# Dealing the rows of w_out four to a partition, and taking h's weights from every fourth column of w_in

## The chip, the cores and the metric

The kernel runs on one core of a Trainium2 chip. A core has a matrix engine (TensorE; the profile writes PE for its matmuls and PEld for its weight loads), a vector engine (DVE), a scalar engine (ACT), GpSimd (POOL), a queue engine that only issues transfers (SP), and 16 DMA engines that carry all transfers. The metric is the device time of one execution in microseconds (us).

## The reference

Two steps follow each other. The first is a gated linear attention over 4 batches, 8 heads, 768 positions and a head size of 48: a state of 48 x 48 per head is faded by a sigmoid gate, receives the outer product of k and v, and is read with q. The second is a feed-forward layer whose activation is a ratio of polynomials, on the 3072 x 384 rows that the first one gives.

```python
f = 1.0 / (1.0 + np.exp(-f_logit))
for t in range(S):
    state = f[:, :, t, :, None] * state + np.einsum('bhd,bhe->bhde', k[:, :, t], v[:, :, t])
    y[:, :, t] = np.einsum('bhd,bhde->bhe', q[:, :, t], state)
...
h = x @ w_in                       # 3072 x 384 by 384 x 2048
h2 = h * h
P = a[0] + a[1] * h + a[2] * h2 + a[3] * h2 * h
Q = 1.0 + np.abs(b[0]) * np.abs(h) + np.abs(b[1]) * h2
out = (P / (Q + 1e-06)) @ w_out    # 2048 x 384
```

The 2048 columns of h (the ff dimension) are independent of each other up to the last product, which sums over them. Any dealing of them to blocks and partitions gives the same output if w_in and w_out follow it alike.

## The kernel before, in words

The work is cut into 12 units of 256 positions (4 batches times 3 chunks). A unit goes through the attention part (steps ef, ls, cs, A, xa, T, sc, mk, yi, yb, ic, si, st, ye) and gives x, 256 tokens by 384, transposed, in bf16. Then the feed-forward part runs on it:

- h (line 480): 16 blocks of 128 ff columns. For each block three matmuls run over the 384 rows of w_in (three tiles of 128). The weights are 128 columns of w_in, the moving operand is x with 256 columns. A step h takes four blocks, thus 12 matmuls, into one PSUM slot; 12 units give 48 steps and 576 matmuls.
- hy (line 492, ACT) brings four blocks from PSUM to SBUF as bf16. The polynomials are made of it by DVE and ACT (sq, sa, ab, p1, p2, pm, tv, zv, gm, and the reciprocal rq), and some of their additions by DMAs that GpSimd issues and that add into their destination (zd, line 514, into z; ta, line 543, into g).
- o (line 560): 16 blocks again. The weights are 128 tokens of g for one ff block, the moving operand is the 384 columns of w_out for the same block. 384 matmuls in all.
- oe (line 568) scales the result, so (line 577) stores it.

All elementwise work treats the ff columns alike, so which column lies in which block or on which partition does not matter to it.

The order of all steps is written out by hand in the string ORDER; each engine runs its own instructions in that order and waits on semaphores for what it needs from others. Marks such as `!m3` and `^m3` tie a step behind another one. There are four PSUM slots; the `@` numbers name the slot.

Both weight matrices stay in SBUF in bf16 and are loaded once by GpSimd's queue, which converts them from float32 on the way: w_in by eight transfers (wi, line 218), w_out by four (wo, line 224). A wo step brings four blocks, thus 512 rows of w_out. In ORDER they stand as wo 8 12, then later wo 4 8, wo 12 16 and wo 0 4, all always in whole groups of four blocks. Before the change, partition p of block m holds row 128 m + p of w_out, so one transfer is, for each of the 128 partitions, four separate runs of one row (384 values). Block m of h takes the packed columns 128 m to 128 m + 127 of w_in.

Of the kernel before, what the change touches and what calls it, by code (L numbers as in the profile page):

```python
# [104 lines left out]
def _at(t, dims, off=0):  # L105

    return bass.AP(tensor=t.tensor, offset=t.offset + off, ap=[t.ap[0]] + [list(d) for d in dims])
# [3 lines left out]
def kernel(  # L111
# [15 lines left out]
    P = 128  # L127
    HP = H // 2
    DM = H * D
    d_ff = moe_w_in.shape[1]  # L130
# [36 lines left out]
    w_in_sb = consts.tile([P, KD, d_ff], BF16, name="w_in_sb")  # L167
# [22 lines left out]
    def unit(n):  # L190
        if n not in units:
            c, b = divmod(n, B)
            units[n] = dict(n=n, c=c, b=b, qk=qkp[n % 2], ls=lsp[n % 2], vm=vmp[n % 2])
        return units[n]
# [5 lines left out]
    def slot(i, shape, dtype, name):  # L200
        return slots[i].tile(shape, dtype, name=name, tag="s")
# [19 lines left out]
                                        ap=[[d_ff, 32], [32 * d_ff, KD], [1, n]]))  # L221

    def load_w_out(m0, m1):
        return nc.gpsimd.dma_start(out=w_out_sb[:, m0:m1, :],
                            in_=moe_w_out[m0 * P:m1 * P, :].rearrange("(ko ki) n -> ki ko n", ki=P))

    def load_ab(what, qu="a"):
        dst, src = (a_sb, moe_a) if what == "a" else (b_sb, moe_b)
# [19 lines left out]
    def const_z(i):  # L248
        if i < 2:
            nc.vector.memset(lsp[i][:, :, :, D:E], 0.0)  # L250
            nc.vector.memset(qkp[i].rearrange("p x i h d -> p (x i h) d")[:, :, D:E], 0.0)
            nc.vector.memset(vmp[i][:, :, :, 16:32], 0.0)
        elif i == 2:
            nc.vector.memset(ind, 0.0)
            for j in range(UB):
                nc.vector.memset(ind[R * j:R * j + R, j, :], 1.0)
        elif i == 4:
            return nc.vector.memset(zz, 0.0)
        else:
            nc.vector.memset(hsel, 0.0)  # L260
            for r in range(2):
                nc.vector.memset(hsel[E * r:E * r + E, :, :, 1 - r], 1.0e4)
# [212 lines left out]
    def h(n, m0, m1, sl):  # L475
        s = unit(n)
        t = s["hp", m0] = slot(sl, [P, 4, NT], F32, "hp")
        for m in range(m0, m1):
            for kk in range(KD):
                nc.tensor.matmul(t[:, m - m0, :].rearrange("f (j t) -> f j t", j=UB),  # L480
                                 w_in_sb[:, kk, m * P:(m + 1) * P], s["x"][:, :, kk, :],
                                 start=(kk == 0), stop=(kk == KD - 1))

    def big(s, key):
# [94 lines left out]
    def behind(i, mark):  # L579
        tc.add_manual_dep(i.ins, marks[mark].ins.name,  # L580
                          mybir.DependencyInfo(mybir.DependencyClass.Sync, mybir.DependencyReason.DATA),
                          reason="begins behind it")

    steps = dict(ld=load, wi=load_w_in, wo=load_w_out, ab_=load_ab, cu=const_u, ci=const_i, cm=const_m,
                 cz=const_z, fa=coef_a, fb=coef_b, fr=coef_r, tab=tab, dm=dm, ef=ef, ls=ls, cs=cs, A=A, xa=xa, T=T, Te=Te,
                 sc=sc, mk=mk, vm=vm, yi=yi, yb=yb, ic=ic, si=si, ye=ye, st=st, h=h, hy=hy, sq=sq, sa=sa, ab=ab,
                 zv=zv, zd=zd, rq=rq, p1=p1, p2=p2, pm=pm, ta=ta, tv=tv, gm=gm, o=o, oe=oe, so=store)
    for step in ORDER.replace("\n", ";").split(";"):
# [41 lines left out]
```

## Time and profile before

| | |
|---|---|
| median of 3 runs | 220.51 us (218.54 to 227.84) |
| the profiled execution | 219.54 us |
| its span, first to last instruction | 217.8 us |
| TensorE matmuls busy | 194.5 us, 2901 instructions |
| TensorE weight loads busy (beside the matmuls) | 138.5 us, 2902 instructions |
| DVE busy | 190.6 us |
| ACT busy | 187.5 us |
| GpSimd busy | 78.8 us |
| matmuls of h (line 480) | 576, 70.9 us |
| weight loads of h | 576, 55.7 us |
| matmuls of o (line 560) | 384, 69.2 us |
| four transfers of w_out | 384 KB each in SBUF, 8.4 us from issue to landing in the median |

Busy time is the time that an engine's instructions cover. A matmul's shown length contains latency that overlaps with the next one, so a row's mean is longer than the distance from one matmul to the next; the distance is read from rows that put several together. The loads of weights run beside the matmuls and have a row of their own. For a transfer the profile gives the time that the issuing engine is occupied and, separately, the time from issue to landing.

### The profile page before, as it was taken

The page shows a single profiled execution, that of the slowest core. Times are in us where ns is not written, and L with a number is a line of the kernel's source. Part 1 is how long each engine was busy: PE and PEld are TensorE (multiplying, and loading weights), DVE is VectorE, ACT ScalarE, POOL GpSimd, SP SyncE. Part 2 cuts the span into 40 slices and gives each one's busy share as a digit, 9 for nine tenths or more (in the row PEclk, how much of TensorE's full clock was granted, in tenths as well). Part 3 has the DMA queues.
Part 4 walks back from the last instruction along what each step waited for, and adds up shares of the span by engine and source line. Part 5 has one row for each costly group of instructions (what it writes and reads, how often), then busy time and mean ns, then how long its engine had stood idle before and what let it go on. Part 6 is the DMA issues. An engine that isn't in the chain of part 4 may idle for free.

```text
span 217.8 us, 6636 instructions
## 1 busy us (share of the span) xinstructions
PE 194.5 (89%) x2901; PEld 138.5 (64%) x2902; DVE 190.6 (88%) x243; ACT 187.5 (86%) x178; POOL 78.8 (36%) x98
## 2 busy tenths in 40 slices
PE   1397699699988899999999999999999999999791
PEld 0355478477756766666678668768677757765440
DVE  4178549999999999999999999999999999979960
ACT  3863639979989999999999999999999999998921
POOL 7050724116394074070260055193553414132000
PEclk9999889999999999999999999999999999999999
DMA  6999997599899979999999999999999999999722
GB/s 171 232 313 168 253 240 189 66 297 182 217 187 178 163 113 200 223 213 191 253 197 164 257 241 243 210 193 204 215 204 199 221 199 215 207 205 199 158 72 72
DMA packets 61820, 43.15 MB, mean 198 GB/s; under 512 B 51424, under 2 KB 56544, under 8 KB 61792
## 3 DMA queue, kind: packets, MB, share of 16 engines
q0 software_dynamic: 20528, 23.86, 66.9%
q1 hardware_dynamic: 41264, 18.88, 33.2%
q8 instruction: 22, 0.36, 0.6%
q14 instruction: 6, 0.05, 0.1%
HBM read 25.17 MB, written 4.72 MB: 137 GB/s over the span
## 4 chain that ended last, share of the span: by engine, by line
PE 54%; DVE 18%; DMA 13%; ACT 8%; issue 4%; POOL 1%; SPq 0%; DVEq 0%; ACTq 0%
PE op L560 19%; PE hp L480 19%; PE y L394 5%; DMA w_in_sb<-in_moe_w_in_dram 4%; DVE g L539 4%; DMA g<-hy 4%; DMA z<-h 4%; PE tp L350 4%; DVE g L551 3%; PE cs L309 3%; DVE scm L381 2%; DVE hy L534 2%; PE sc L373 2%; DMA f<-in_f_logit_dram 2%; ACT A L331 2%
## 5 line engine op out<-in xcount | busy, mean ns | idle before, releaser
L480 PE MATMUL hp<-x,w_in_sb 128*128 128x256 bf16 x576 | 70.9, 276 | 2.4 <-ACT x L457 1.0
L560 PE MATMUL op<-w_out_sb,g 128*128 128x384 bf16 x384 | 69.2, 326 | 1.8 <-DVE g L551 1.8
L480 PEld LDWEIGHTS <-w_in_sb 128*128 128x128 bf16 x576 | 55.7, 99 | 12.8 <-issue 3.1
L492 ACT CAST hy<-hp 128x1024 bf16<-128x1024 f32 x48 | 48.0, 1026 | 6.9 <-PE hp L480 6.9
L560 PEld LDWEIGHTS <-g 128*128 128x128 bf16 x384 | 35.3, 98 | 25.0 <-DVE g L551 3.2
L519 ACT ACTIVATE qi<-z 128x2048 bf16<-128x2048 bf16 (+1 forms) x20 | 45.3, 2267 | 2.1 <-DMA z<-h 1.9
L543 POOL DMA_DIRECT2D g<-hy x15 | 15.3, 1017 | 50.6 <-DVE hy L534 23.1
L381 DVE TENSOR_TENSOR scm<-sc,mask 128x1024 bf16<-128x1024 f32 x24 | 28.9, 1216 | 4.0 <-PE sc L373 3.9
L551 DVE TENSOR_TENSOR g<-g,qi 128x2048 bf16<-128x2048 bf16 (+1 forms) x22 | 28.8, 1315 | 2.1 <-DMA g<-hy 1.6
L539 DVE TENSOR_TENSOR g<-g,h 128x2048 bf16<-128x2048 bf16 (+1 forms) x22 | 30.4, 1394 | 0.0
L514 POOL DMA_DIRECT2D z<-h x20 | 21.6, 1078 | 21.7 <-DVE z L505 11.6
L501 ACT ACTIVATE h<-hy 128x2048 bf16<-128x2048 bf16 x14 | 27.1, 1934 | 0.0
L331 ACT ACTIVATE A<-cs 128x768 f32<-128x768 f32 (+3 forms) x26 | 19.2, 773 | 1.7 <-PE cs L317 1.6
L534 DVE TENSOR_SCALAR hy<-hy,a_sb 128x2048 bf16<-128x2048 bf16 x24 | 19.9, 834 | 0.3
L336 POOL TENSOR_TENSOR qkp<-k,A 128x384 bf16<-128x384 f32 x12 | 12.1, 1012 | 19.8 <-DVE sig L274 8.0
L529 DVE TENSOR_SCALAR g<-hy,a_sb 128x2048 bf16<-128x2048 bf16 (+1 forms) x22 | 18.9, 862 | 0.2 <-PE op L560 0.2
L505 DVE TENSOR_SCALAR z<-hy 128x2048 uint16<-128x2048 uint16 (+1 forms) x23 | 16.1, 707 | 2.6 <-ACT hy L492 2.6
L212 POOL DMA_DIRECT2D v<-in_v_dram x12 | 12.5, 1042 | 15.4 <-DVE qkp L336 7.0
L309 PE MATMUL cs<-lsp,Ui 128*128 128x384 bf16 (+1 forms) x39 | 11.1, 344 | 6.2 <-ACT lsp L299 6.2
L360 ACT COPY T<-tp 128x1024 f32<-128x1024 f32 (+1 forms) x13 | 12.5, 963 | 4.5 <-PE y L394 3.3
L568 ACT ACTIVATE osb<-op 128x768 f32<-128x768 f32 (+1 forms) x13 | 9.9, 762 | 6.1 <-PE op L560 5.6
L394 PE MATMUL y<-scm,v 64*32 64x128 bf16 x384 | 13.2, 218 | 2.0 <-DVE scm L381 2.0
(71 smaller groups left out, 247.4 us busy)
## 6 DMA issues: line engine op xcount, KB each, us to landing
z<-h POOLq DMA_DIRECT2D x20, 512.0 KB, 7.8
g<-hy POOLq DMA_DIRECT2D x15, 512.0 KB, 7.2
f<-in_f_logit_dram SPq DMA_DIRECT2D x11, 384.0 KB, 5.4
k<-in_k_dram SPq DMA_DIRECT2D x11, 384.0 KB, 4.9
q<-in_q_dram SPq DMA_DIRECT2D x11, 384.0 KB, 7.6
out_dram<-osb SPq DMA_DIRECT2D x22, 192.0 KB, 4.2
v<-in_v_dram POOLq DMA_DIRECT2D x12, 192.0 KB, 7.3
w_in_sb<-in_moe_w_in_dram POOLq DMA_DIRECT2D x8, 192.0 KB, 9.0
```

The costliest lines, as they stand in the source:

```text
L331: nc.scalar.activation(t, s["cs", a0][:, :, 0:n1], AF.Exp, scale=1.0 if x else -1.0)
L381: return nc.vector.tensor_mul(t, s["sc", g].rearrange("s r a i t -> s (r a) (i t)"), mb)
L394: nc.tensor.matmul(s["y"][32 * a:32 * a + 32, j, kk * C:kk * C + C].rearrange("e (i t) -> e i t", i=2), lhsT, rhs, start=(j, a) not in s[" ...
L480: nc.tensor.matmul(t[:, m - m0, :].rearrange("f (j t) -> f j t", j=UB), w_in_sb[:, kk, m * P:(m + 1) * P], s["x"][:, :, kk, :], start=(kk ...
L492: nc.scalar.copy(fl(big(s, "hy"), m0, m1), fl(s["hp", m0], 0, m1 - m0))
L501: return nc.scalar.activation(fl(big(s, "h2"), m0, m1), fl(big(s, "hy"), m0, m1), AF.Square)
L514: return nc.gpsimd.dma_start(out=fl(big(s, "z"), m0, m1), in_=fl(big(s, "h2"), m0, m1), accum_op=ALU.add)
L519: return nc.scalar.add_instruction(mybir.InstActivation(name=nc.get_next_instruction_name(), func=AF.Reciprocal, ins=[nc.scalar.lower_ap(f ...
L534: return nc.vector.tensor_scalar(fl(big(s, "hy"), m0, m1), fl(big(s, "hy"), m0, m1), a_sb[:, 1:2], a_sb[:, 0:1], op0=ALU.mult, op1=ALU.add)
L539: return nc.vector.tensor_mul(fl(big(s, "g"), m0, m1), fl(big(s, "g"), m0, m1), fl(big(s, "h2"), m0, m1))
L551: return nc.vector.tensor_mul(fl(big(s, "g"), m0, m1), fl(big(s, "g"), m0, m1), fl(big(s, "qi"), m0, m1))
L560: nc.tensor.matmul(s["op", g][:, j, 0:DM], big(s, "g")[:, m, C * j:C * j + C], w_out_sb[:, m, :], start=(s["on", j] == 1), stop=(s["on", j ...
```

## The change

A transfer of w_out now gives each partition four successive rows, which lie together in memory as one run of 1536 values. Within a group of four blocks starting at row 512 G, partition p holds rows 512 G + 4 p to 512 G + 4 p + 3, and block m of the group is the row with remainder m mod 4. For h to agree, block m takes the columns of w_in that end in the same remainder: 128 columns of the group's 512, every fourth one. So the weights of h's matmuls are read with a step of four elements, 8 bytes. w_in lies in SBUF as before, its transfers are the same, and ORDER is the same.

```diff
     def load_w_out(m0, m1):
+
         return nc.gpsimd.dma_start(out=w_out_sb[:, m0:m1, :],
-                            in_=moe_w_out[m0 * P:m1 * P, :].rearrange("(ko ki) n -> ki ko n", ki=P))
+                            in_=moe_w_out[m0 * P:m1 * P, :].rearrange("(ki ko) n -> ki ko n", ki=P))
...
                 nc.tensor.matmul(t[:, m - m0, :].rearrange("f (j t) -> f j t", j=UB),
-                                 w_in_sb[:, kk, m * P:(m + 1) * P], s["x"][:, :, kk, :],
+                                 _at(w_in_sb, [[4, P]], kk * d_ff + 512 * (m // 4) + m % 4), s["x"][:, :, kk, :],
                                  start=(kk == 0), stop=(kk == KD - 1))
```

The helper `_at(t, dims, off)` builds an access pattern on a tile: the tile's partitions, then the given pairs of step and count, from the given offset. An empty line is added, so lines behind it have numbers higher by one in the kernel after.

## The prediction

> **What bounds the kernel now.** I read the page's first and fourth part, then cut the span into stretches, then read the stretch that is full, line by line.
>
> ```profile
> span 217.8 us, 6636 instructions
> ...
> PE 194.5 (89%) x2901; PEld 138.5 (64%) x2902; DVE 190.6 (88%) x243; ACT 187.5 (86%) x178; POOL 78.8 (36%) x98
> ```
>
> The profiled execution took 219.54 us by the times: its span of 217.8 and 1.7 around it. I make the sum against 219.54; the median of the three runs, 220.51, lies 1.0 above it. Three engines have nearly the same load, so the page alone does not name a bound. The view by stretches does; its columns are the stretch, its length and each engine's busy time.
>
> ```profile
> core 0: us, PE busy (x) PEld busy (x) DVE busy (x) ACT busy (x) POOL busy (x), PEclk, DMA share, GB/s
> 0.00:36.00 36.00, 24.48 (x449) 17.21 (x453) 19.89 (x54) 20.64 (x30) 13.04 (x28) 0.95 1.09 226
> 36.00:76.00 40.00, 34.53 (x653) 27.60 (x644) 39.36 (x47) 37.04 (x38) 17.47 (x19) 1.00 1.03 186
> 76.00:176.00 100.00, 100.00 (x1501) 70.84 (x1500) 98.40 (x111) 98.58 (x88) 41.08 (x45) 1.00 1.06 207
> 176.00:217.80 41.80, 35.52 (x316) 22.83 (x314) 32.99 (x35) 31.28 (x25) 7.19 (x7) 0.99 0.79 165
> ```
>
> From 76 to 176 TensorE never rests, and VectorE and ScalarE rest 1.5% of the time. From 36 to 76 VectorE is the fullest and TensorE has 5.5 us free. So whatever lengthens TensorE's work after 76 is paid in full, and an earlier arrival before 76 helps only where an engine stands waiting for it. The same view of the line of h's matmuls alone tells how much of TensorE's work the change touches.
>
> ```profile
> core 0: us, PE busy (x) PEld busy (x), PEclk, DMA share, GB/s
> 36.00:76.00 40.00, 20.02 (x168) 15.89 (x168) 1.00 1.03 186
> 76.00:176.00 100.00, 36.19 (x300) 28.60 (x300) 1.00 1.06 207
> ```
>
> Of 576 matmuls of h, 300 run in the full stretch.
>
> **Part one: h's weight loads take every fourth column.** Each of the 576 loads still brings 128 columns of bf16 from 128 partitions, but they lie 8 bytes apart where they were packed. The matmuls, what they stream and where they write are unchanged. The cost of a load with a step is not in this trace: every load of the kernel reads packed columns. So first: how much room does a load have? Here are rows of groups (mean ns of one ahead of the bar's right side) and of the order in time (start, length, count).
>
> ```profile
> L480 PE MATMUL hp<-x,w_in_sb 128*128 128x256 bf16 x576 | 70.9, 276 | 2.4 <-ACT x L457 1.0 <-DMA w_in_sb<-in_moe_w_in_dram 0.8 <-DVE state L464 0.4
> L480 PEld LDWEIGHTS <-w_in_sb 128*128 128x128 bf16 x576 | 55.7, 99 | 12.8 <-issue 3.1
> L394 PEld LDWEIGHTS <-v 64*32 64x32 bf16 x384 | 8.7, 91 | 5.3 <-issue 4.6
> L373 PEld LDWEIGHTS <-T 48*64 48x64 bf16 x384 | 6.2, 106 | 6.9 <-issue 4.8 <-ACT T L360 1.1 <-ACT hy L492 0.5
> L317 PEld LDWEIGHTS <-lsp 128*128 128x128 bf16 x96 | 3.4, 97 | 0.0
> ```
> ```profile
> 71.39 0.27 PEld L317 LDWEIGHTS <-lsp 128*128 128x128 bf16 x8
> 71.42 0.34 PE L317 MATMUL cs<-ind,lsp 128*128 128x4 bf16 x8
> 71.59 2.52 PEld L480 LDWEIGHTS <-w_in_sb 128*128 128x128 bf16 x24
> 71.62 2.78 PE L480 MATMUL hp<-x,w_in_sb 128*128 128x256 bf16 x24
> ```
>
> 24 matmuls of h take 2.78 us, the last of them 0.276, so one starts every (2.78 - 0.276) / 23 = 109 ns. The loads run beside them, one ahead. Line 317 shows how fast packed loads can follow each other: its matmuls stream 4 columns only, and eight loads take 0.27 us, so one starts every (0.27 - 0.097) / 7 = 25 ns, though each is shown as 97 ns long. The shown length is mostly latency that overlaps; the interval is what must fit. A load of h therefore uses 25 of its 109 ns.
>
> Bounds for the interval of a load with the step: from below 25 ns, no change (a step can't save anything, for as many columns are read). From above by the rows: loads of 64 columns take 106 ns and of 32 columns 91, that is 0.47 ns for each further column, yet 128 packed columns take 97 to 99: full loads must take several columns at once. Without that, 128 columns would need 128 x 0.47 = 60 ns. The step spreads the same columns over four times the bytes; if each load paid fourfold for that, it would be 4 x 25 = 99 ns with the fast form and 4 x 60 = 240 ns without. Three of these four values (25, 60, 99) lie below 109. I take 50 ns, twice the packed one, because the nearest row (line 317, the same 128 x 128 load) says 25 and I know of no row that makes it shorter. Inside a block of 12 matmuls that costs nothing: the 109 ns of the matmul ahead hide it. That cover is gone at the start of a block behind short work. There are 48 blocks; if half of them expose 25 ns, that is 24 x 25 ns = **+0.6 us**. The ends: 0, and 48 x (107 - 25) = 3.9 us for a load that only just fits.
>
> The rule that bears on this is in the Trainium skill, "SBUF — State Buffer", section "Door 1: The DMA port swizzle": memory lines are 16 bytes, and two reads in each line are needed for full bandwidth. Columns 8 bytes apart are exactly two to a line, so by that rule the load stays at 25 ns and this part costs 0.0 rather than 0.6 us. No run here shows a load with any step, so the trace neither agrees nor disagrees.
>
> **Part two: w_out's four transfers.** Each was 128 partitions x 4 runs of 384 values; each is now 128 runs of 1536 values. Bytes are equal; 2048 pieces become 512.
>
> ```profile
> L224 POOL DMA_DIRECT2D w_out_sb<-in_moe_w_out_dram x4: 807/904/941, 60.2 to 66.2; - x4
> ...
> DMA to landing us min/median/max: 7.3/8.4/10.1
> ```
> ```profile
> q0 software_dynamic: 20528, 23.86, 66.9%
> q1 hardware_dynamic: 41264, 18.88, 33.2%
> ```
> ```profile
> 56.01 7.70 DMA z<-h
> 63.71 0.02 issue
> 63.73 3.29 ACT qi L519
> ```
> ```profile
> ACT qi L519 <- DMA z<-h: 0.9, 1, 0.9
> ...
> PE sv L439 <- POOL qkp L336: 0.2, 1, 0.2
> ```
>
> The first two rows are those of the transfers; the next are the queues of the whole run (packets, MB, share of 16 engines' span); then the chain of waits and the waits between 54 and 80. A packet of the hardware queue costs 0.332 x 16 x 217.8 / 41264 = 28 ns with 457 bytes in it, so the saving for one packet less is between 0 and 28 ns: 1536 fewer give 0 to 43 us of engine time, 0 to 2.7 us on each of 16 engines, spread over the transfers between 60 and 76. Who waits for it? Nobody in w_out's own rows: the first matmul that reads it starts at 76.2, and the last issue, at 66.2 with a landing of 8.4, is in by 75. What shares the engines is the transfer that adds h's square to z, issued at 56.01 and landed 7.70 later; ScalarE waited 0.9 us for it. So the most that can come off the path is 0.9 us there and, if GpSimd issues faster, the 0.2 us that TensorE waited for GpSimd's product at 62. In the other direction, a packet four times as large makes a transfer beside it wait longer: the software queue's mean is 0.669 x 16 x 217.8 / 20528 = 114 ns, four times that is 0.45 us. Ends -1.1 and +0.45; I take **-0.2 us**, near nothing, since most of z's 7.70 us were over when w_out's first transfer was issued at 60.2. What is late next after 63.7 is ScalarE itself: it works through to the matmuls at 76.
>
> **GpSimd's issue.** Four issues of 0.81 to 0.94 us. Rows with fewer and with more pieces:
>
> ```profile
> L218 POOL DMA_DIRECT2D w_in_sb<-in_moe_w_in_dram x8 | 4.5, 572 | 0.0
> L212 POOL DMA_DIRECT2D v<-in_v_dram x12 | 12.5, 1042 | 15.4 <-DVE qkp L336 7.0 <-DVE vmp L388 5.4 <-PE y L394 3.0
> ```
> ```profile
> 64.70 2.44 POOL L224 DMA_DIRECT2D w_out_sb<-in_moe_w_out_dram  x3
> 66.97 1.06 POOL L212 DMA_DIRECT2D v<-in_v_dram  x1
> 76.43 0.92 POOL L543 DMA_DIRECT2D g<-hy  x1 [8.40 <-DVE hy L534]
> ```
>
> 96 pieces took 572 ns, 1024 took 1042, so 128 may take 0.3 us less than 512 do. Three of the four issues stand ahead of a rest of 8.4 us, where nothing is gained; the first is in the 0.2 us above. No wait is added anywhere and every queue keeps its order.
>
> Sum: 219.54 + 0.6 - 0.2 = **219.9 us**.
>
> **Rivals.**
> *The loads become the bound* (slower). If the interval of a load with the step goes over 109 ns, TensorE pays the rest 300 times in the full stretch at least and 576 times at most. That is the point from which it decides. If the loads lose the fast form and also stop overlapping, the length decides: 91 + 96 x 0.47 = 136 ns, +27 ns, +8 to +16 us, 228 to 235 us. At 240 ns it is +131 ns, +39 to +75 us, 259 to 295 us. For it: no load here shows a step, and four times the bytes are passed over. Against it: the room of 84 ns over today's interval.
> *The starts of blocks are exposed in full*: loads of 100 to 107 ns, +2 to +3.9 us, 221.5 to 223.4 us. For it: TensorE is full. Against it: many blocks follow long matmuls, which hide the first load too.
> *w_out's smaller packet count is worth its upper end* (faster): z lands 0.9 us earlier, GpSimd 0.2, and the loads cost nothing: 218.4; if the saved 2.7 us on each engine all reached the path, 216.8.
> *The change doesn't do what it says*: the transfers are cut again into small packets. Then w_out gives nothing; 219.5 to 220.1, inside the forecast.
>
> The Trainium skill has a rule for the first rival in "TensorE: Matmul & The Clock Gate", section "Weight-path perf modes": the fast load of 128 columns stays in use for column steps from -1,023 to 1,024. By that rule the rival falls away. This trace can't show it, since all its steps are 1, so I keep the rival's chance.
>
> **How the numbers follow.** The forecast with its own spread (218.4 to 221.5) has 0.61; exposed starts 0.13; the gain at its upper end (216.8 to 218.4) 0.09; loads as the bound 0.14; and 0.03 that a reordering of waits that I don't see gains over 2%. 2% is 4.4 us, about what a measurement here can tell from no change: faster 0.03, within 0.82, slower 0.15 (0.14 and 0.01 for exposed starts beyond their bound). The range goes from the gain's end, 216.8, to the end of the exposed starts, 223.4, and on to 225, because the runs of before have a median 1.0 above the execution I sum against; left out are the loads as bound and the unseen gain, 0.17. The bounds of 228 to 295 belong to that left-out case.
>
> **What would show it.** The rows of h's weight loads: a mean near 99 ns, or up to 136, with 24 matmuls still in about 2.78 us, confirms part one; 24 matmuls in more than 3 us shows the loads as the bound, and TensorE's row from 76 on stretches with it. The page's count of packets under 2 KB falls by 2048 and w_out's landing comes under 8.4 us if part two does what it says. ScalarE's wait for z near 63 shows whether that reached anyone. I'd be wrong if a load with a step takes over 109 ns, or if a wait moves somewhere after 176, where TensorE is not full and the order is fine.

## The result, and the profile after

The kernel after takes 228.5 us in the median of 4 runs (228.1 to 231.82), the kernel before 221.05 in the median of 4 (218.54 to 227.84; one run more than in the table above). The ratio is 1.043, with a 95% interval of 1.037 to 1.048: slower; by the medians it is 1.034. Ratios with an interval go by the runs near the fastest of their kernel, and as one run of the kernel before was far ahead of its others in the first comparison below (215.16 us, then 217.59 to 221.29), the medians of all runs stand beside them. The profiled execution took 228.76 us, of which 227.1 are its span; before it was 219.54 and 217.8. So 9.3 us of span are to be found. All lines behind the added empty one have numbers higher by one: h's matmuls are L481, w_out's transfers L225.

The page's first part, the engines' rows of the 40 slices, and the count of packets, of the kernel after:

```profile
span 227.1 us, 6636 instructions
...
PE 195.6 (86%) x2902; PEld 145.4 (64%) x2902; DVE 190.6 (84%) x243; ACT 187.7 (83%) x178; POOL 77.1 (34%) x98
...
PE   1497109988998899999999999999999999999891
...
DVE  4186601599999999999999999999999999998960
ACT  3873400997998999999999999999999999997921
...
PEclk9999755999999999999999999999999999999999
...
DMA packets 60284, 43.15 MB, mean 190 GB/s; under 512 B 51424, under 2 KB 54496, under 8 KB 60256
```

TensorE is busy 1.1 us longer and DVE and ACT are not, and the 6.9 us more of weight loads run beside the matmuls: no engine has 9 us more to do. But in the fifth and sixth slice (a slice is 5.7 us, so 23 to 34 us) TensorE does nearly nothing, and ACT nothing in the sixth and seventh. A stall of that size is missing in the kernel before. The same rows of its page, and its count of packets, for comparison:

```profile
PE   1397699699988899999999999999999999999791
...
ACT  3863639979989999999999999999999999998921
...
DMA packets 61820, 43.15 MB, mean 198 GB/s; under 512 B 51424, under 2 KB 56544, under 8 KB 61792
```

What ends the stall is in the order in time on TensorE around it, first of before and then of after (start, length, what, and in brackets the idle time ahead and what ended it):

```profile
24.36 0.51 PE L439 MATMUL sv<-v,qkp 64*128 64x96 bf16 x16
25.65 2.65 PE L480 MATMUL hp<-x,w_in_sb 128*128 128x256 bf16 x12 [0.77 <-DMA w_in_sb<-in_moe_w_in_dram]
```

```profile
23.85 0.52 PE L440 MATMUL sv<-v,qkp 64*128 64x96 bf16 x16
34.52 2.72 PE L481 MATMUL hp<-x,w_in_sb 128*128 128x256 bf16 x12 [10.16 <-DMA w_in_sb<-in_moe_w_in_dram]
```

The first matmul of h starts at 34.52 instead of 25.65, 8.9 us later, and it waits for a transfer of w_in, a matrix whose loading the diff does not touch. GpSimd's rows in the order in time, here of the kernel after, show which: the eight transfers of w_in are issued in two groups of four. The view of their line gives the time from issue to landing.

```profile
14.29 2.28 POOL L218 DMA_DIRECT2D w_in_sb<-in_moe_w_in_dram  x4
21.60 0.91 POOL L212 DMA_DIRECT2D v<-in_v_dram  x1 [5.02 <-DVE vmp L389]
22.50 2.23 POOL L218 DMA_DIRECT2D w_in_sb<-in_moe_w_in_dram  x4
```

```profile
DMA to landing us min/median/max: 6.6/8.8/10.2
```

The first group carries columns 1024 to 2047 and its last issue ends at 16.6; with at most 10.2 us it is in before 27. The second group carries columns 0 to 1023; its last issue begins at 24.2 and lands by 34.4. The first step of h (ORDER's `h 0 8 12`) reads columns 1024 to 1535, all of the first group. Yet it starts when the second group is in. The program as built says why. These are its weight loads of h that wait for transfers, with the names of the semaphores, of before and of after. Seven names stand for eight transfers: DMASW2 counts one transfer of each group, and the kernel after waits there for its second count.

```
before   h 0 8 12  Ldweights w_in_sb [waits DMASW4, DMASW5, DMASW3, DMASW2]
         h 0 4 8   Ldweights w_in_sb [waits DMASW2, DMASW7, DMASW1, DMASW0]
after    h 0 8 12  Ldweights w_in_sb [waits DMASW4, DMASW3, DMASW5, DMASW2, DMASW7, DMASW1, DMASW0]
         h 0 4 8   Ldweights w_in_sb
```

The waits are not written in the kernel; the layer that builds the program derives them from what each instruction reads and writes. A read of w_in with a step is taken there to overlap with all of the tile's eight transfers, though its columns all lie in four of them. In the program as built (not run) with steps of 2 and 8, and with a plain stepped slice instead of the helper, the wait is the same; with the helper and a step of 1 it is the four of before.

From the first matmul of h to the end of the span, before took 217.8 - 25.65 = 192.2 us and after 227.1 - 34.52 = 192.6. So 8.9 of the 9.3 us lie ahead of it. No other wait of TensorE's loads and matmuls for a transfer or an engine differs between the two programs, but that `h 0 4 8`, whose four transfers are awaited earlier now, waits no more.

The rest of the profile after answers the prediction's other rows. The loads' lengths, and w_out's transfers:

```profile
L481 PEld LDWEIGHTS <-w_in_sb x576: 110/113/147, 34.5 to 205.0; 128*128 128x128 bf16 x192
...
L481 PE MATMUL hp<-x,w_in_sb x576: 269/273/418, 34.5 to 205.1; 128*128 128x256 bf16 x192
```

```profile
L225 POOL DMA_DIRECT2D w_out_sb<-in_moe_w_out_dram x4: 608/670/715, 69.8 to 75.4; - x4
...
DMA to landing us min/median/max: 6.3/7.9/9.9
```

And one piece of 24 matmuls of h at the same place of the order (behind y), of before and of after:

```profile
84.87 2.89 PE L480 MATMUL hp<-x,w_in_sb 128*128 128x256 bf16 x24
```

```profile
94.10 2.90 PE L481 MATMUL hp<-x,w_in_sb 128*128 128x256 bf16 x24
```

A load is 113 ns long in the median where it was 98, but 24 matmuls take the same time to 0.01 us.

### The profile page after: what moved, and what is told of

Same layout as the page of the kernel before. It is cut to its first block, busy times and chain, and to the rows that moved or that the text cites. A ratio compares the mean times of both kernels' runs of the same rounds, so it can differ in the third digit from the quotient of the medians.

```text
span 227.1 us, 6636 instructions
## 1 busy us (share of the span) xinstructions
PE 195.6 (86%) x2902; PEld 145.4 (64%) x2902; DVE 190.6 (84%) x243; ACT 187.7 (83%) x178; POOL 77.1 (34%) x98
## 2 busy tenths in 40 slices
DMA packets 60284, 43.15 MB, mean 190 GB/s; under 512 B 51424, under 2 KB 54496, under 8 KB 60256
## 4 chain that ended last, share of the span: by engine, by line
PE 54%; DVE 19%; DMA 13%; ACT 7%; issue 4%; SPq 0%; DVEq 0%; ACTq 0%
PE hp L481 18%; PE op L561 18%; PE y L395 6%; DMA w_in_sb<-in_moe_w_in_dram 4%; DVE g L540 4%; PE tp L351 4%; DMA g<-hy 3%; DMA z<-h 3%; DVE scm L382 3%; PE cs L310 3%; DVE g L552 3%; PE sc L374 2%; DVE hy L535 2%; DVE qkp L337 2%; DMA f<-in_f_logit_dram 2%
## 5 line engine op out<-in xcount | busy, mean ns | idle before, releaser
L481 PE MATMUL hp<-x,w_in_sb 128*128 128x256 bf16 x576 | 71.8, 279 | 11.6 <-DMA w_in_sb<-in_moe_w_in_dram 10.2
L481 PEld LDWEIGHTS <-w_in_sb 128*128 128x128 bf16 x576 | 62.4, 115 | 16.7 <-issue 12.2
L493 ACT CAST hy<-hp 128x1024 bf16<-128x1024 f32 x48 | 48.0, 1023 | 16.7 <-PE hp L481 16.6
L544 POOL DMA_DIRECT2D g<-hy x15 | 14.2, 946 | 51.7 <-DVE hy L535 23.4
L515 POOL DMA_DIRECT2D z<-h x20 | 19.7, 985 | 21.5 <-DVE z L506 7.7
L465 DVE TENSOR_TENSOR state<-sv,A 128x384 bf16<-128x384 f32 x20 | 10.9, 548 | 10.9 <-PE sv L450 10.9
L337 POOL TENSOR_TENSOR qkp<-k,A 128x384 bf16<-128x384 f32 x12 | 12.6, 1050 | 19.3 <-ACT A L332 10.3
L337 POOL TENSOR_TENSOR qkp<-q,A 128x384 bf16<-128x384 f32 x10 | 10.5, 1048 | 18.4 <-ACT A L332 16.7
```

The source lines that it names most:

```text
L337: i = (nc.gpsimd if eng == "p" else nc.vector).tensor_mul(s["qk"][:, x, :, hh, 0:D], s["qk"[x]][:, hh].rearrange("p h i d -> p i h d"), s[ ...
L493: nc.scalar.copy(fl(big(s, "hy"), m0, m1), fl(s["hp", m0], 0, m1 - m0))
L515: return nc.gpsimd.dma_start(out=fl(big(s, "z"), m0, m1), in_=fl(big(s, "h2"), m0, m1), accum_op=ALU.add)
```

## The experiments

Two theories stood against each other. A: the wait for all of w_in is the whole loss. B: the weight loads with a step cost it, a little at each; 576 x 15 ns is 8.6 us, which happens to be the right size. Besides, w_out's transfers could have cost something. In the comparisons below the kernel before ran 11 times beside the first four kernels (219.78 us in the median) and 17 other times beside the last three (219.86). By the ratio with its interval only early_w_in is clearly slower by the 2% that counts as a change; the other five are rated unclear, though the whole interval of wait_only lies above 1.04.

**two_tiles**: the whole change, with w_in in two tiles of 1024 columns, so that a block waits for its own half.

```diff
-    w_in_sb = consts.tile([P, KD, d_ff], BF16, name="w_in_sb")
+    w_in_sb = [consts.tile([P, KD, d_ff // 2], BF16, name=f"w_in_sb{i}") for i in range(2)]
...
-        return nc.gpsimd.dma_start(out=w_in_sb[32 * a:32 * a + 32, :, m0 * P:m1 * P],
+        return nc.gpsimd.dma_start(out=w_in_sb[m0 // 8][32 * a:32 * a + 32, :, m0 % 8 * P:(m0 % 8 + m1 - m0) * P],
...
-                                 _at(w_in_sb, [[4, P]], kk * d_ff + 512 * (m // 4) + m % 4), s["x"][:, :, kk, :],
+                                 _at(w_in_sb[m // 8], [[4, P]], kk * (d_ff // 2) + 512 * (m % 8 // 4) + m % 4), s["x"][:, :, kk, :],
```

> The whole change, with w_in in two tiles of 1024 columns each instead of one of 2048, so that the first block of h can wait for the four transfers of its own half alone. Theory A (the first weight load of h waits for all eight transfers of w_in instead of four, and this is the whole loss): h's first matmul starts near 25.6 us again instead of 34.5, and the time is 0.99 to 1.005 of before. Theory B (the weight loads with a step cost it: their rows are 15 ns longer, 113 against 98, and 576 x 15 ns is 8.6 us): h starts near 25.6 but the time stays near 1.04 of before, 228 us, with the gap spread over the span.

Measured: 220.13 us in the median of 6 (219.2 to 220.66) beside 219.78 of before: 1.002 by the medians, 1.014 (1.005 to 1.023) by the given ratio. In its order in time the first step of h, and below it the view of its line, with loads as long as in the kernel after:

```profile
26.11 2.72 PE L481 MATMUL hp<-x,w_in_sb 128*128 128x256 bf16 x12 [0.61 <-DVE scm L382]
```

```profile
L481 PEld LDWEIGHTS <-w_in_sb x576: 110/113/148, 25.4 to 196.3; 128*128 128x128 bf16 x192
```

The step is in all 576 loads, and by the profiled executions 8.6 of the 9.3 us are gone (218.5 us of span against 227.1). B, which needs 1.04, falls: even the upper end of the interval is 1.023. At the same granted clock, the share of full speed that TensorE was given, the two kernels take the same time: the six runs of two_tiles had 0.987 to 0.990 and took 219.2 to 220.66 us, and the five runs of before at 0.988 and 0.989 took 219.53 to 220.49.

**wait_only**: the kernel before, with the wait alone. Each transfer of w_in is kept in a list, and the first matmul of h is made to begin behind all of them.

```diff
+                if (n, m, kk) == (0, 8, 0):
+                    for d in made_wi:
+                        tc.add_manual_dep(i.ins, d.ins.name,
+                                          mybir.DependencyInfo(mybir.DependencyClass.Sync, mybir.DependencyReason.DATA),
+                                          reason="waits for all of w_in")
```

> The kernel before with packed weights and w_out as it was; only the first matmul of h is also made to wait for all eight transfers of w_in. Theory A: 1.035 to 1.05 of before, about 228 to 230 us, with ScalarE standing about 14.6 us before its first copy of h. Theory B: the weights are packed, so at most the wait itself shows and it is absorbed later; 1.00 to 1.02.

Measured: 229.65 us (227.73 to 230.63) beside 219.78: 1.045 by the medians, 1.057 (1.046 to 1.068) by the given ratio. ScalarE stood 14.3 us before its first copy of h, where theory A said 14.6. Weights packed, w_out as before, and the whole loss is there:

```profile
34.60 1.65 PE L482 MATMUL hp<-x,w_in_sb 128*128 128x256 bf16 x7 [9.62 <-DMA w_in_sb<-in_moe_w_in_dram]
```

**wout_only** and **step_only**: the two parts of the change, each alone. The first takes the kernel before and the new line of w_out's transfers; the second takes two_tiles with the old line. In both, the sum over ff pairs columns of g with other rows of w_out, so the output is another one for the same work.

```diff
-                            in_=moe_w_out[m0 * P:m1 * P, :].rearrange("(ko ki) n -> ki ko n", ki=P))
+                            in_=moe_w_out[m0 * P:m1 * P, :].rearrange("(ki ko) n -> ki ko n", ki=P))
```

> The kernel before with the four transfers of w_out dealt out as in the change and h's weights packed as before (the sum over ff then pairs g with other rows of w_out, so the output is another one; the work is the same). Theory A and B: 0.995 to 1.003 of before, as the saved packets reach nobody but a 0.9 us wait of ScalarE. If w_out's transfers were the cause: above 1.02.

> Weights of h with the step of four from two tiles, w_out's transfers as before (the pairing of ff is again another one, the work the same). Theory A: 1.000 to 1.008 of before: the loads are longer in the rows but hidden. Theory B: 1.03 to 1.045.

Measured, beside 219.78 of before: wout_only 220.24 us (217.92 to 222.33), 1.002 by the medians and 1.013 (0.9995 to 1.027) by the given ratio; step_only 220.59 (218.99 to 222.19), 1.004 and 1.016 (1.004 to 1.029). Neither part costs anything near 4%, and w_out's part gains nothing that shows. ScalarE's wait for z, which was to shrink from 0.9 us, is 1.1 us in wout_only and 0.6 in the kernel after. Whether the step costs some tenths of a per cent these runs don't settle: the runs of before differ by more among themselves, and the interval of step_only goes up to 2.9%.

**packed_two_tiles**: the control for two_tiles, the kernel before with the same two tiles and packed weights (the first two lines of the edit of two_tiles, and `w_in_sb[m // 8][:, kk, m % 8 * P:(m % 8 + 1) * P]` for the weights).

> The kernel before with w_in in two tiles and nothing else: 0.995 to 1.005 of before, about 219.8 us, since its first load of h waits for the same four transfers as in one tile. If the split itself moves the time, two_tiles doesn't stand for the change without the wait.

Measured: 220.14 us in the median of 12 (216.44 to 223.81) beside 219.86 of before: 1.001 by the medians, 1.007 (0.997 to 1.016) by the given ratio. The split moves nothing that shows, and two_tiles (220.13, beside another set of runs of before) is at the same time.

**early_w_in**: the kernel after in one tile, with the second four transfers issued right behind the first four. The wait for all eight stays; what it waits for comes earlier.

```diff
-... wi 3 8 16; xa 1 1 2 4; wi 1 8 16
+... wi 3 8 16; xa 1 1 2 4; wi 1 8 16; wi 2 0 8; wi 3 0 8; wi 0 0 8; wi 1 0 8
...
-... yb 0 2 4; wi 2 0 8; sc 1 1 @0; ld 5 f; ye 0 s; sc 1 0 @3; wi 3 0 8; mk 1 1 !m2
-ls 3; ic 1 @1; wi 0 0 8; A 2 1; wi 1 0 8; mk 1 0 !m4; ...
+... yb 0 2 4; sc 1 1 @0; ld 5 f; ye 0 s; sc 1 0 @3; mk 1 1 !m2
+ls 3; ic 1 @1; A 2 1; mk 1 0 !m4; ...
```

> The whole change with w_in in one tile, so that the first load of h still waits for all eight transfers, but the second four are issued right behind the first four, near 16 to 20 us instead of 22.5 to 24.7. Theory A says that the time follows the landing of the last one: h's first matmul at the landing, 26 to 30 us, and the time 219.9 plus what that is later than 26, thus 220 to 224 us, between before and after. If the loads with a step were the loss it would stay at 228.

Measured: 225.37 us (223.91 to 225.97) beside 219.86: 1.025 by the medians, 1.028 (1.022 to 1.034) by the given ratio; the profiled execution took 224.62. It lies between, as theory A says, though the median is 1.4 us above the upper end that I had given.

```profile
30.12 2.72 PE L481 MATMUL hp<-x,w_in_sb 128*128 128x256 bf16 x12 [5.24 <-DMA w_in_sb<-in_moe_w_in_dram]
```

Five profiled executions side by side (us):

| kernel | first matmul of h | span | span less that start |
|---|---|---|---|
| before | 25.65 | 217.8 | 192.2 |
| two_tiles | 26.11 | 218.5 | 192.4 |
| early_w_in | 30.12 | 222.9 | 192.8 |
| after | 34.52 | 227.1 | 192.6 |
| wait_only | 34.60 | 227.8 | 193.2 |

The start moves over 9 us, the rest over 1. The time follows the start about one for one.

**probe**: what a load with a step costs by itself. two_tiles with a tail of 160 matmuls behind the work: groups of 16 that stream 4 columns with weights at a step of 1, 2, 4, 8 and 16, each behind 16 that stream 512. It adds work, so its time means nothing.

```diff
+        def run(w, r):
+            for i in range(16):
+                nc.tensor.matmul(t[:, 0, 0:r], w(i), zz[:, 0:r], start=True, stop=True)
+        run(lambda i: _at(w_in_sb[0], [[1, P]], i), 512)
+        run(lambda i: _at(w_in_sb[0], [[1, P]], 16 * i), 4)
...
+        run(lambda i: _at(w_in_sb[0], [[1, P]], i), 512)
+        run(lambda i: _at(w_in_sb[0], [[4, P]], 16 * i), 4)
...
```

> The kernel of two_tiles with a tail of its own: five groups of 16 matmuls that stream 4 columns only and read 128 weight columns with a step of 1, 2, 4, 8 and 16 columns, each group behind 16 matmuls of 512 columns. The distance between two of the short matmuls is the interval of a weight load. If the 15 ns that h's loads grew by are paid in the interval: 25 ns for step 1, 40 for step 4. If they are latency alone: 25 for both. The forecast took 50 for step 4. For steps 8 and 16 (16 and 32 bytes) one theory says no change over step 4, another doubles it; over 109 would show the rival that I priced.

The view by stretches of the probe's line, two stretches with one start within each group (the stretch, its length, busy time and, in brackets, the number of matmuls and of loads). How many more loads the longer one holds gives the distance between loads:

```profile
216.86:216.90 0.04, 0.04 (x6) 0.04 (x5) 1.00 0.00 0
216.86:217.10 0.24, 0.24 (x14) 0.24 (x13) 1.00 0.00 0
220.70:220.74 0.04, 0.04 (x5) 0.04 (x4) 1.00 0.00 0
220.70:220.94 0.24, 0.24 (x13) 0.24 (x12) 1.00 0.00 0
224.56:224.64 0.08, 0.08 (x6) 0.08 (x5) 1.00 0.00 0
224.56:224.96 0.40, 0.40 (x16) 0.40 (x15) 1.00 0.00 0
228.60:228.80 0.20, 0.20 (x7) 0.20 (x6) 1.00 0.00 0
228.60:229.20 0.60, 0.60 (x14) 0.60 (x13) 1.00 0.00 0
233.00:233.20 0.20, 0.20 (x7) 0.20 (x6) 1.00 0.00 0
233.00:233.60 0.60, 0.60 (x14) 0.60 (x13) 1.00 0.00 0
```

Steps of 1 and 2: 8 loads in 0.20 us, 25 ns. Step of 4: 10 in 0.32 us, 32 ns. Steps of 8 and 16: 7 in 0.40 us, 57 ns. These are whole counts, good to some 5 ns; the start that the trace holds for each load gives 25, 25, 33, 61 and 61 ns in the median, and I go by these. None comes near the 109 ns of a matmul of h. I had expected 25 or 40 for the step of 4; it is between. A step of 16 is not twice a step of 8.

## Why the prediction was wrong, point by point

The forecast was 219.9 us in a range of 216.8 to 225.0; it came to 228.5.

**The step that failed** is in "GpSimd's issue": "No wait is added anywhere and every queue keeps its order." The second half holds. The first half was an inference from it: I looked at which instructions stand where, and not at which transfers each one waits for. The change adds waits ahead of one of the 5804 weight loads and matmuls on TensorE's queue, the first load of h: TensorE stands 10.16 us there instead of 0.77. Everything on TensorE behind it stands too, and that is where ScalarE's first copy of h and the state updates were waiting. The view of waits of the kernel after has them all in a few rows:

```profile
ACT hy L493 <- PE hp L481: 16.6, 5, 14.6
...
DVE state L465 <- PE sv L450: 10.9, 3, 9.9
PE hp L481 <- DMA w_in_sb<-in_moe_w_in_dram: 10.2, 1, 10.2
```

The profile before had a warning that I didn't use: the groups' row of h's matmuls, quoted in the prediction, holds "DMA w_in_sb<-in_moe_w_in_dram 0.8". h's first matmul already had w_in's landing as its last wait, with no slack, and the second group is issued 8.6 us behind the first (14.03 against 22.61). Any tie to it would have been priced at about 9 us. None of the rivals had this mechanism: the one on the slow side was priced for the right part, the weights of h, but for the time of the loads. The chance of 0.03 for waits that I don't see was put on the faster side, and the only moved wait that I named as a sign of being wrong was to come after 176 us; this one came at 24.

**Part one, the loads**, was right in what mattered. The interval was put at 50 ns between bounds of 25 and 240, hidden under 109; the probe gives 33, and by the medians step_only and two_tiles cost 0.4% and 0.2%, less than the runs of before differ among themselves. The mean shown length, 115 ns, lies in the 99 to 136 that I named. Exposed starts of blocks: 0.6 us taken, which no run shows or excludes, as it is under 0.3% of the time; the same piece behind y takes 2.90 us instead of 2.89, so for that start 0.01 us rather than 0.025.

**The rival that the loads become the bound** fell, and with it the 0.14 of chance that made up nearly all of the slower side. The outcome was slower, but by another cause; that 228.5 us lies in the 228 to 235 given for this rival is chance.

**Part two, w_out**, was right in its signs: packets under 2 KB fell by 56544 - 54496 = 2048, just as many as the old transfers had, and the median landing went from 8.4 to 7.9 us. Nobody gained anything that shows: wout_only is at 1.002 by the medians, and the term of -0.2 us is too small for these runs to tell from nothing. The rival that the transfers are cut again fell too.

**GpSimd's issue** was put 0.3 us shorter per transfer; the median went from 904 to 670 ns, 0.23. It is hidden, as said.

**The sum** of +0.4 us for all but the wait meets the 0.4 by which the rest of the span after h's first matmul grew (192.2 to 192.6). The agreement is closer than the terms deserve, as two_tiles and early_w_in give 0.2 and 0.6 for about the same rest.

A small part of the loss may be the clock. In the 10 us behind the first matmul of h the granted clock was 0.84 before and 0.77 after:

```profile
25.60:36.00 10.40, 10.34 (x189) 8.05 (x192) 7.07 (x14) 5.34 (x7) 2.52 (x4) 0.84 1.09 218
```

```profile
34.50:45.00 10.50, 10.47 (x164) 7.98 (x168) 4.04 (x6) 4.77 (x6) 0.00 (x0) 0.77 0.38 98
```

That is 0.16 x 10.4 = 1.7 us of TensorE's clock lost there before and 0.23 x 10.5 = 2.4 us after: at most 0.7 us more, inside the 192.6 us. The stall doesn't start it: in both executions the clock is 0.50 from 26 to 28 us, while TensorE is busy before and stands still after, and it is 1.00 again from 30 us before and from 40 us after. What lowers it was not tested.

The two rules of the Trainium skill: "SBUF — State Buffer", section "Door 1: The DMA port swizzle", wants two reads in each 16-byte line. The probe agrees in the form: little is lost with two to a line (33 ns against 25), and at one to a line the interval goes to 61 and doesn't grow for a longer step. By the letter of the rule the step of 4 would have cost nothing; the measurement says 8 ns. "TensorE: Matmul & The Clock Gate", section "Weight-path perf modes", says that the fast load stays in use for such steps. The 25 ns at a step of 2 and 33 at a step of 4 agree, well under the 60 that I had worked out for loads without it; the 61 ns of the steps of 8 and 16 don't tell which of the two, a slower read or a lost fast form, it is.

## What to carry to other kernels

When an edit changes how an instruction reads a buffer, compare what it waits for, not only where it stands: the layer that places the waits may take a read with a step for a read of everything that was ever loaded into that tile, and the first reader then waits for the last transfer. Giving each separately loaded part its own tile takes that away without touching the work. And price it from the profile before: a wait that already ends last with no slack, on a matrix loaded in groups, can grow by the distance between the groups, here 8.6 us foreseen by the issues and 8.9 measured at the start of h.

## What the runs showed that I had not expected

A weight load of 128 bf16 columns starts every 25 ns with a step of 1 or 2 columns, 33 ns with 4, and 61 ns with 8 or 16, while its shown length goes from 96 (step of 1) over 116 (step of 4) to 169 ns (step of 8): the length overstates the cost by far, and its growth of 15 ns per load, 8.6 us over all of h, was worth nothing in the time that these runs could show.

And 9 us of a stall near the start were not made up at all later: with VectorE busy for 39.36 of the 40 us from 36 on, and three engines nearly full from 76 to 176, the span grew by 0.9 to 1.1 us for each microsecond by which h began later (218.5, 222.9 and 227.1 us for 26.11, 30.12 and 34.52).
